# A re-planned instruction order, 45 fewer idle matmuls and three output stores in halves, in a fused RWKV attention and SMELU feed-forward kernel

## The chip, the core and the metric

The kernel runs on one core of one Trainium2 chip as a single launch. The metric is the device time of one execution in microseconds (us). The kernel before has a median of 182.87 us over 5 runs (182.36 to 184.13).

## What is computed

A recurrent attention without softmax (RWKV) over 4 batches, 8 heads, 768 steps and 48 channels per head, then a feed-forward layer with the SMELU activation over the 3072 rows of 384 channels that come out of it.

```python
batch, n_heads, seq, head_dim = (4, 8, 768, 48)
n_tokens, d_model, d_ff = (3072, 384, 2048)
...
for t in range(S):
    cur = np.einsum('bhd,bhe->bhde', u[None] * kt, vt)
    y[:, :, t] = np.einsum('bhd,bhde->bhe', rt, state + cur)
    state = w[None, :, :, None] * state + np.einsum('bhd,bhe->bhde', kt, vt)
...
h = x @ w_in
g = np.where(pos, h, np.where(neg, 0.0, (h + beta) ** 2 / (4.0 * beta)))
return (g @ w_out).astype(np.float32)
```

Here pos is h >= 1, neg is h <= -1, and beta is 1. All inputs and the output are float32.

## The kernel before

**Units.** The sequence is cut into 6 chunks of 128 steps. A chunk of one batch is a unit, so there are 24 units, numbered chunk by chunk, and unit i belongs to batch i % 4. Two units make a feed-forward block m of 256 rows (12 blocks).

**Names.** Each piece of work has a short name, used below and in the order string. For unit i:

- ld:K:i, ld:R:i, ld:V:i load 192 KB each with DMAs issued by SyncE's queue (SP).
- Kw and Rw multiply K and R by tables of decay powers and write both into one bf16 tile RKW (line 282). KU1 and KU2 form u*K*R, and dg sums it per head (line 297); Vb is V in bf16; VD is V times dg.
- trp transposes RKW on TensorE (line 306) and trc copies the result out; from unit 8 on tr does it by a DMA.
- at computes the scores A (line 322), mk masks their two halves on VectorE (line 326), y is the matmul with V (lines 334 to 343), x its copy out of PSUM, xp and xT its transpose and copy, and xs a sum of squares.
- st is the update of the state (line 378), Ta, Td and Tb its addition, decay and bf16 copy.

For a block m: L1:m:n is a group of the first feed-forward matmul (line 401) and sm the squared activation that takes it from PSUM (line 412, ScalarE). For blocks 0 and 1 the two units are done apart, as L1:m:n:u. L2:m:u:n is two matmuls of the second layer (line 432), oc copies unit u's output from PSUM, so stores it (line 447). The last unit's output (L2:11:1) is done in two column halves, and its second half is stored by ScalarE's queue.

**Weights.** w_in and w_out come as four slices each, loaded by GpSimd's (POOL's) own DMA queue with a cast to bf16: gi:0 to gi:3 and go:0 to go:3. li:z and lo:z stand for their landing and issue nothing. Before each of these loads a copy of one element on POOL (lines 460, 465, 470) waits for a certain other load: gi:0 to gi:3 for K1, R1, V1 and K2, go:0 to go:3 for K3, R3, V3 and K4. L1:0:2 needs slice li:2, L2:m:u:4 and 5 need lo:2, L2:m:u:6 and 7 need lo:3.

**Order.** The string ORDER (lines 16 to 89) holds all pieces of work in one list. A loop at the end (line 638) emits them in that order, so that each engine's and each queue's own sequence is what the list leaves for it; engines wait for each other by semaphores. A suffix such as @DVE picks another engine for a piece. The costs and due times that stand beside each op in the code take no part in the run. The token warm*n emits n matmuls of an identity matrix with itself (line 240), whose result nobody reads; there are 126 of them.

**End.** The last thing that SP does is to wait for the semaphores of its eight DMA lanes, one after the other (line 650). DMAs issued by SP and ScalarE take the eight lanes in turn.

Of the kernel before, what the change touches and what calls it, by code (L numbers as in the profile page):

```python
# [689 lines left out]
```

## Time and profile before

| | |
|---|---|
| median of 5 runs | 182.87 us |
| the profiled execution | 182.68 us, of which the profile's span is 180.8 us |
| TensorE (PE) busy | 168.3 us, 93% of the span |
| VectorE (DVE), ScalarE (ACT), GpSimd (POOL) busy | 120.4, 105.8 and 108.5 us |
| mean granted TensorE clock | 0.997 |
| idle matmuls (line 240) | 126, 10.6 us of busy time |
| from 39 to 100 us | PE busy 61.0 of 61 us, DVE 53.1, POOL 53.7, ACT 42.8 |
| DMA engines' mean share in the first 40 us | 0.84 to 1.19 |

How to read it: the span runs from the first instruction of the program to the last. A row of the timeline has its start, its length, the engine, the line, the operation, the tiles it writes and reads, how many instructions were merged, and in brackets how long the engine had been idle before and what ended that. Times of matmuls are pipelined: the time from one start to the next is shorter than the duration of one. PEld is the weight load in TensorE, SPq the instruction queue of SyncE.

### The profile page before, as it was taken

How to read it: one execution, taken by the hardware profiler on the slowest of the kernel's cores; microseconds unless marked ns; L12 is line 12 of the kernel's file. 1: busy time of each engine (PE TensorE's matmuls, PEld its weight loads, DVE VectorE, ACT ScalarE, POOL GpSimd, SP SyncE). 2: the span in 40 equal slices, each digit the busy share in tenths (PEclk: the TensorE clock that was granted, in tenths of full speed). 3: DMA queues.
4: the chain of work that ended last, by engine and by line, in shares of the span. 5: the costliest groups of instructions: out<-in, count | busy, mean ns of one | idle time of the engine just before them, and what ended most of it. 6: DMA issues, size and time to landing. Idle time of an engine off the chain costs nothing.

```text
span 180.8 us, 4899 instructions
## 1 busy us (share of the span) xinstructions
PE 168.3 (93%) x1891; PEld 129.7 (72%) x1891; DVE 120.4 (67%) x330; ACT 105.8 (59%) x225; POOL 108.5 (60%) x151
## 2 busy tenths in 40 slices
PE   5987587999999999999999999999999999999980
PEld 3876477767878777787778777777777776887670
DVE  2276762459996899879868999889869675100220
ACT  3406296526859549588737567777956551674300
POOL 7797389754999797999988998922950000000000
PEclk9999999999999999999999999999999999999998
DMA  5999979999989999996999788999943023020131
GB/s 95 221 190 206 194 113 219 205 175 187 232 202 206 202 198 237 199 189 91 247 202 181 172 135 183 224 184 204 200 113 99 4 54 98 4 86 0 39 108 49
DMA packets 103424, 27.79 MB, mean 154 GB/s; under 512 B 96481, under 2 KB 103394, under 8 KB 103394
## 3 DMA queue, kind: packets, MB, share of 16 engines
q1 hardware_dynamic: 99538, 24.16, 66.8%
q0 software_dynamic: 3712, 3.15, 11.2%
q8 instruction: 17, 0.28, 0.6%
q14 instruction: 13, 0.11, 0.2%
q10 hardware_dynamic: 144, 0.10, 0.2%
HBM read 20.65 MB, written 4.72 MB: 140 GB/s over the span
## 4 chain that ended last, share of the span: by engine, by line
PE 80%; SPq 12%; DMA 4%; issue 0%; DVE 0%; ACT 0%
PE o_p L432 35%; PE h_p L401 32%; SPq L278 12%; PE A L322 4%; DMA R<-in_r_dram 4%; PE y L337 2%; PE y L334 2%; PE st L378 2%; PE tr L306 1%; PE xp L362 1%; DVE RKW L282 0%; PE y L343 0%; SPq L243 0%; PE n_p L488 0%; PE o_p L240 0%
## 5 line engine op out<-in xcount | busy, mean ns | idle before, releaser
L412 ACT ACTIVATE gT<-h_p 128x512 bf16<-128x512 f32 x96 | 56.8, 596 | 39.3 <-PE h_p L401 37.5
L401 PE MATMUL h_p<-xT,w_in_sb 128*128 128x256 bf16 (+1 forms) x672 | 75.1, 257 | 2.6 <-DMA w_in_sb<-in_moe_w_in_dram 2.2
L432 PE MATMUL o_p<-w_out_sb,gT 128*128 128x384 bf16 (+1 forms) x400 | 75.9, 320 | 0.0
L401 PEld LDWEIGHTS <-w_in_sb 128*128 128x128 bf16 x672 | 56.9, 98 | 13.0 <-DMA w_in_sb<-in_moe_w_in_dram 2.4
L432 PEld LDWEIGHTS <-gT 128*128 128x128 bf16 x400 | 36.4, 98 | 15.6
L326 DVE TENSOR_TENSOR AT<-A,umask 128x512 bf16<-128x512 f32 x48 | 31.4, 685 | 8.9 <-PE A L322 8.7
L354 DVE SCALAR_TENSOR_TENSOR x<-Vb,dg,y 128x48 bf16<-128x48 bf16 x144 | 26.7, 258 | 5.3 <-PE y L337 5.2
L282 POOL TENSOR_TENSOR RKW<-K,Winv 128x384 bf16<-128x384 f32 x21 | 22.0, 1051 | 3.3 <-DMA K<-in_k_dram 1.7
L182 DVE COPY o_sb<-o_p 128x384 f32<-128x384 f32 (+1 forms) x20 | 10.6, 542 | 19.9 <-PE o_p L432 19.7
L293 POOL TENSOR_TENSOR KU<-KU,R 128x384 f32<-128x384 f32 x20 | 20.3, 1017 | 5.0 <-DMA R<-in_r_dram 2.3
L182 ACT CAST Tbd<-T 48x192 bf16<-48x192 f32 x40 | 13.9, 349 | 14.7 <-DVE T L386 9.5
L290 POOL TENSOR_TENSOR KU<-K,u_bc 128x384 f32<-128x384 f32 x22 | 22.0, 1003 | 0.0
L372 ACT ACTIVATE x<-x 128x384 bf16<-128x384 bf16 x24 | 12.5, 520 | 4.9 <-DVE x L354 3.5
L282 POOL TENSOR_TENSOR RKW<-R,Wpow 128x384 bf16<-128x384 f32 x14 | 14.0, 1000 | 0.3 <-DMA R<-in_r_dram 0.3
L182 POOL CAST Vb<-V 128x384 bf16<-128x384 f32 x22 | 11.3, 517 | 4.7 <-PE h_p L401 2.5
L297 DVE TENSOR_REDUCE dg<-KU 128x8 f32<-128x384 f32 x24 | 12.9, 544 | 0.7 <-POOL KU L293 0.5
L282 DVE TENSOR_TENSOR RKW<-R,Wpow 128x384 bf16<-128x384 f32 x10 | 7.8, 779 | 7.6 <-DMA R<-in_r_dram 7.6
L384 DVE TENSOR_TENSOR T<-T,st 48x192 f32<-48x192 f32 x32 | 11.2, 350 | 2.5 <-PE st L378 1.9
L389 POOL TENSOR_TENSOR T<-T,wc 128x192 f32<-128x192 f32 x16 | 9.1, 568 | 6.1 <-DVE T L384 6.0
L240 PE MATMUL w_p<-ident 128*128 128x128 bf16 x120 | 10.6, 253 | 0.0
L240 PEld LDWEIGHTS <-ident 128*128 128x128 bf16 x126 | 9.6, 116 | 0.3
L322 PEld LDWEIGHTS <-RK 48*128 48x128 bf16 x192 | 5.4, 94 | 6.0 <-issue 4.9
(74 smaller groups left out, 145.8 us busy)
## 6 DMA issues: line engine op xcount, KB each, us to landing
K<-in_k_dram SPq DMA_DIRECT2D x24, 192.0 KB, 3.8
R<-in_r_dram SPq DMA_DIRECT2D x24, 192.0 KB, 4.1
V<-in_v_dram SPq DMA_DIRECT2D x24, 192.0 KB, 3.9
out_dram<-o_sb SPq DMA_DIRECT2D x23, 192.0 KB, 2.5
w_in_sb<-in_moe_w_in_dram POOLq DMA_DIRECT2D x4, 384.0 KB, 8.1
w_out_sb<-in_moe_w_out_dram POOLq DMA_DIRECT2D x4, 384.0 KB, 7.7
RK<-RKW SPq DMA_TRANSPOSE x16, 3.5
w_bc<-in_w_dram SPq DMA_DIRECT2D x1, 192.0 KB, 3.6
```

The lines of the kernel that those rows point to most:

```text
L182: (eng.copy if eng is nc.scalar else eng.tensor_copy)(to, src)
L240: mm(spare[0][:, d_out:], ident, ident, start=False, stop=False, skip_group_check=True)
L278: nc.sync.dma_start(out=t[name, i], in_=src[b, :, c * C : (c + 1) * C, :].rearrange("h s d -> s h d"))
L282: at_engine((name + "w", i)).tensor_mul(RKW[i % RING["W"]][:, off : off + H, 0:D], t[name, i], tab)
L290: at_engine(("KU1", i)).tensor_mul(t["KU", i], t["K", i], u3)
L293: at_engine(("KU2", i)).tensor_mul(t["KU", i], t["KU", i], t["R", i])
L297: nc.vector.reduce_sum(t["dg", i], t["KU", i], axis=AX)
L326: nc.vector.tensor_mul(t["AT", i, s], t["A", i][s], umask4)
L354: nc.vector.scalar_tensor_tensor(x[:, h * D : (h + 1) * D], t["Vb", i][:, h, :], t["dg", i][:, h : h + 1], t["y", i][:, h, :], op0=ALU.mul ...
L401: mm(h_p[:, f, :], w_in_sb[:, kk, (nf * n + f) * 128 : (nf * n + f + 1) * 128], xT[m][:, :, kk, :] if u_ is None else xT[m][:, u_, kk, :], ...
L412: nc.scalar.activation(g, h_p, AF.Square, bias=0.5, scale=0.5)
L432: mm(t["o", m, u, part_], t["g", m][:, f, u * C : (u + 1) * C], w_out_sb[:, f, e], start=(f == 0), stop=(f == nN - 1),)
```

## The change

- The whole ORDER is another one. It holds the same pieces of work; 15 of them sit on another engine (Kw:0, Kw:1, KU1:3, KU2:3 and KU2:22 go from POOL to DVE, Rw:9 from DVE to POOL, VD:2 from DVE to POOL, trc:3 from ACT and xT:0 from ACT to DVE, Vb:4, Vb:15, Vb:17 from POOL to ACT, and oc:4:0, oc:5:1 and oc:11:0 from DVE to ACT).
- 81 idle matmuls stand in place of 126: 7 and 30 before the first transposes (12 and 41 before), 2, 11, 9 and 17 up to the first group of layer 1 (11, 12, 17, 2), none around at:1 (7 and 7), 5 ahead of L1:0:1:1 (2 and 9), and none ahead of L2:0:1:4 (6).
- The stores of units 20, 21 and 22 go out as two DMAs of half the columns each.
- The tile dg has 12 buffers in place of 4.
- Scores of two units in one piece of work are provided for from unit PAIR = 24 on; there is no unit 24, so no instruction comes from it.

```diff
 ORDER = """
-w u ld:K:0 ld:K:1 ln warm*12 ub tab:K ld:R:0 Kw:0 wt uc ld:V:1 tab:R KU1:0 dec ld:R:1 gi:0 ld:V:0 Rw:0 KU2:0
-warm*41 trp:0 ld:R:2 trc:0@DVE gi:1 li:0 dg:0 warm*11 at:0 Vb:0 mk:0:1 VD:0@POOL st:0 mk:0:0 gi:2 ld:K:2
-Ta:0:1 warm*12 y:0 Ta:0:0 Tb:0:1 Rw:1 Tb:0:0 ld:V:2 Kw:1 x:0@DVE warm*17 xp:0 xs:0 li:2 gi:3 trp:1 xT:0
-trc:1 Kw:2@DVE warm*2 L1:0:0:0 Rw:2 KU1:1@DVE sm:0:0:0 li:1 warm*7 at:1 KU2:1 mk:1:0 KU1:2 warm*7 L1:0:2:0
-dg:1 mk:1:1 li:3 Vb:1 sm:0:2:0 trp:2 KU2:2@DVE trc:2 VD:1 st:1 dg:2 Vb:2 L1:0:1:0 Ta:1:0 ld:K:3 y:1 VD:2
-sm:0:1:0 at:2 Ta:1:1 x:1 ld:K:4 mk:2:1 st:2 Tb:1:0 xs:1 L1:0:3:0 mk:2:0 ld:R:3 go:0 Tb:1:1 xp:1 Ta:2:0
-sm:0:3:0 Ta:2:1 ld:V:3 warm*2 y:2 xT:1 Kw:4 x:2@DVE Tb:2:0 ld:R:4 Tb:2:1 go:1 warm*9 L1:0:1:1 xs:2 xp:2 lo:0
-sm:0:1:1 L1:0:0:1 go:2 L1:0:2:1 sm:0:0:1 Rw:4 xT:2 L1:0:3:1 Kw:3 sm:0:2:1 lo:1 trp:4 sm:0:3:1 Rw:3@POOL
-L1:1:0:0 trc:4@DVE L1:1:1:0 KU1:3 sm:1:0:0 L2:0:1:0 sm:1:1:0 L2:0:0:0 lo:2 go:3 at:4 L2:0:1:1 mk:4:1 KU1:4
-L1:1:2:0 mk:4:0 trp:3 sm:1:2:0 KU2:4 L2:0:1:2 lo:3 L2:0:1:3 trc:3 L1:1:3:0 KU2:3 dg:4 sm:1:3:0 Vb:3 dg:3
-warm*6 L2:0:1:4 L2:0:1:5 ld:K:5 L2:0:0:1 VD:3@POOL L2:0:0:2 at:3 ld:V:4 L2:0:0:3 mk:3:0 L2:0:0:4 st:3
-L2:0:1:6 mk:3:1 ld:K:6 L2:0:1:7 KU1:5 L2:0:0:5 Ta:3:0 L2:0:0:6 Ta:3:1 ld:R:5 Tb:3:0 L2:0:0:7 Vb:4 oc:0:1 y:3
-Tb:3:1 VD:4 L2:1:0:0 ld:V:5 x:3 L2:1:0:1 oc:0:0 xs:3 L2:1:0:2 Kw:5@DVE st:4 ld:R:6 y:4 Rw:5 xp:3 x:4
...
-sm:11:7 L2:10:1:6 oc:10:0 L2:10:1:7 L2:11:1:0:1 oc:10:1 L2:11:0:0 L2:11:0:1 L2:11:0:2 L2:11:0:3 so:10:0
-L2:11:1:0:0 L2:11:1:1:1 L2:11:1:2:1 L2:11:0:4 so:10:1 L2:11:0:5 L2:11:0:6 L2:11:0:7 L2:11:1:1:0 L2:11:1:2:0
-oc:11:0 L2:11:1:3:0 L2:11:1:4:0 L2:11:1:5:0 L2:11:1:6:0 L2:11:1:7:0 L2:11:1:3:1 L2:11:1:4:1 oc:11:1:0
-L2:11:1:5:1 L2:11:1:6:1 L2:11:1:7:1 so:11:0 oc:11:1:1 so:11:1:0
+w u ld:K:0 ld:K:1 ln warm*7 ub tab:K ld:R:0 Kw:0@DVE wt uc ld:V:1 tab:R gi:0 dec ld:V:0 KU1:0 ld:R:1 Rw:0
+KU2:0 warm*30 trp:0 li:0 trc:0@DVE Vb:0 dg:0 gi:1 warm*2 at:0 st:0 mk:0:1 VD:0@POOL ld:R:2 mk:0:0 gi:2
+Ta:0:0 ld:K:2 warm*11 y:0 Ta:0:1 Tb:0:0 Rw:1 Tb:0:1 ld:V:2 Kw:1@DVE Vb:1 x:0@DVE warm*9 trp:1 li:2 gi:3 st:1
+xs:0 xp:0 Ta:1:1 trc:1 Rw:2 KU1:2 xT:0@DVE Ta:1:0 li:1 Tb:1:0 KU1:1@DVE warm*17 L1:0:0:0 Kw:2@DVE at:1
+sm:0:0:0 KU2:2@DVE L1:0:2:0 mk:1:0 KU2:1 li:3 dg:2 sm:0:2:0 trp:2 Vb:2 mk:1:1 VD:2@POOL trc:2 dg:1 st:2
+L1:0:1:0 VD:1 ld:K:3 Ta:2:0 sm:0:1:0 at:2 y:1 Tb:2:0 mk:2:1 ld:R:3 x:1 mk:2:0 L1:0:3:0 xs:1 ld:R:4 go:0
+sm:0:3:0 Ta:2:1 ld:K:4 Tb:1:1 xp:1 go:1 y:2 Tb:2:1 xT:1 x:2@DVE ld:V:3 Kw:3 xs:2 warm*5 L1:0:1:1 lo:0 Kw:4
+L1:0:0:1 sm:0:1:1 Rw:4 xp:2 sm:0:0:1 L1:0:2:1 go:2 xT:2 L1:0:3:1 lo:1 sm:0:2:1 Rw:3@POOL trp:4 sm:0:3:1
+L1:1:0:0 trc:4@DVE go:3 L1:1:1:0 sm:1:0:0 KU1:3@DVE trp:3 lo:2 sm:1:1:0 at:4 KU2:3@DVE L2:0:1:0 trc:3@DVE
+KU1:4 L2:0:1:1 L1:1:2:0 mk:4:0 KU2:4 L2:0:0:0 dg:3 sm:1:2:0 lo:3 L1:1:3:0 mk:4:1 VD:3@POOL L2:0:1:2 sm:1:3:0
+L2:0:1:3 dg:4 L2:0:0:1 Vb:3 L2:0:0:2 L2:0:1:4 L2:0:1:5 ld:K:5 at:3 L2:0:0:3 mk:3:1 ld:V:4 L2:0:0:4 L2:0:0:5
+mk:3:0 st:3 L2:0:1:6 ld:K:6 L2:0:1:7 Ta:3:1 KU1:5 L2:0:0:6 Ta:3:0 Tb:3:1 L2:0:0:7 oc:0:1 ld:R:5 Tb:3:0 y:3
...
+L2:10:0:7 sm:11:7 L2:10:1:6 oc:10:0 L2:10:1:7 L2:11:1:0:1 oc:10:1 L2:11:0:0 L2:11:0:1 L2:11:0:2 L2:11:0:3
+so:10:0 L2:11:1:0:0 L2:11:1:1:1 L2:11:0:4 so:10:1 L2:11:0:5 L2:11:0:6 L2:11:1:1:0 L2:11:1:2:1 L2:11:1:2:0
+L2:11:1:3:0 L2:11:0:7 L2:11:1:4:0 L2:11:1:5:0 oc:11:0@ACT L2:11:1:6:0 L2:11:1:7:0 L2:11:1:3:1 L2:11:1:4:1
+oc:11:1:0 L2:11:1:5:1 L2:11:1:6:1 L2:11:1:7:1 oc:11:1:1 so:11:0 so:11:1:0
 """
...
@@ -124,12 +124,13 @@
     nN = d_ff // 128
     nP = nN // 2
     UB = 2
+    SPLIT = (20, 21, 22)
     MT = UB * C
     NB = NU // UB
     NQ = 4
     FQ, TQ = d_ff // NQ, nN // NQ
     LIM = 0.95
-    PE_T, PE_X, PE_D, ONE = 8, 14, 6, 2
+    PE_T, PE_X, PE_D, ONE, PAIR = 8, 14, 6, 2, 24
     mm = nc.tensor.matmul
     AX = mybir.AxisListType.X
 
@@ -293,7 +294,7 @@
         at_engine(("KU2", i)).tensor_mul(t["KU", i], t["KU", i], t["R", i])
 
     def diag(i):
-        t["dg", i] = work.tile([128, H], F32, name="dg", tag="dg", bufs=4)
+        t["dg", i] = work.tile([128, H], F32, name="dg", tag="dg", bufs=12)
         nc.vector.reduce_sum(t["dg", i], t["KU", i], axis=AX)
 
     def vdiag(i):
@@ -444,6 +445,10 @@
     def store(m, u, part_=None, queue=nc.sync):
         c, b = at_of(m * UB + u)
         t0 = b * S + c * C
+        if part_ is None and m * UB + u in SPLIT:
+            for z in range(2):
+                queue.dma_start(out=out[t0 : t0 + C, part(z)], in_=t["o_sb", m, u, part_][:, part(z)])
+            return
         queue.dma_start(out=out[t0 : t0 + C, part(part_)], in_=t["o_sb", m, u, part_])
 
     w_in_src = moe_w_in.rearrange("(ko ki) n -> ki ko n", ki=128)
@@ -507,6 +512,16 @@
 
 
     P, L0 = 13.0, 17.0
+    RTs = {}
+
+
+    def at_key(i):
+        return ("at", i if i < PAIR else i - i % 2)
+
+    def scores_of_two(i):
+        scores(i)
+        scores(i + 1)
+
     op("w", "SP", 0.6, load_w)
     op("u", "SP", 0.1, load_u)
     op("ub", "PE", 1.3, spread_u, ["u"], 0, [("a", ["uc"])])
@@ -545,7 +560,7 @@
         if i < PE_D:
             op(("VD", i), "DVE", 0.5, (vdiag, i), [("dg", i), ("ld", "V", i)], d + 4, [("VD", [("y", i)])], port=True,
                alt={"POOL": (1.0, True)})
-        rk = ("RK", [("at", i)] + [("y", i)] * (c > 0))
+        rk = ("RK", [at_key(i)] + [("y", i)] * (c > 0))
         if pe:
             op(("trp", i), "PE", 0.47, (tr_pe, i), [("Kw", i), ("Rw", i)], d + 2, [("a", [("trc", i)])])
             op(("trc", i), "ACT", 1.02, (tr_copy, i), [("trp", i)], d + 2, [rk], alt={"DVE": (0.68, False)})
@@ -553,9 +568,14 @@
         else:
             op(("tr", i), "SP", 1.6, (tr_dma, i), [("Kw", i), ("Rw", i)], d + 2, [rk], land=3.5)
             RT = ("tr", i)
-        op(("at", i), "PE", 0.45, (scores, i), [RT], d + 3, [("a", [("mk", i, s)]) for s in range(2)])
+        RTs[i] = RT
+        if i < PAIR:
+            op(("at", i), "PE", 0.45, (scores, i), [RT], d + 3, [("a", [("mk", i, s)]) for s in range(2)])
+        elif i % 2:
+            op(at_key(i), "PE", 0.66, (scores_of_two, i - 1), [RTs[i - 1], RT], d + 1,
+               [("a", [("mk", z, s)]) for z in (i - 1, i) for s in range(2)])
         for s in range(2):
-            op(("mk", i, s), "DVE", 0.69, (mask, i, s), [("at", i)], d + 3, [("AT" + str(s), [("y", i)])])
+            op(("mk", i, s), "DVE", 0.69, (mask, i, s), [at_key(i)], d + 3, [("AT" + str(s), [("y", i)])])
         needs = [("mk", i, s) for s in range(2)] + [("Vb", i)]
         needs += [("VD", i)] * (i < PE_D) + [("Tb", i - B, s) for s in range(2) if c > 0]
         op(("y", i), "PE", 0.22 + 0.17 * (c > 0) + 0.19 * (i < PE_D), (ymm, i), needs, d + 5, [("a", [("x", i)])])
```

## The prediction

> **What bounds the kernel now.** I read the page first, then the chain of waits up to 40 us, the busy time by stretches, the waits of TensorE, the timeline of the first 36 us with the DMA landings, and last the instructions at the end.
>
> By stretches (the columns are the busy times of PE, PEld, DVE, ACT and POOL):
>
> ```profile
> 15.00:20.50 5.50, 2.95 (x47) 2.45 (x47) 4.11 (x9) 2.61 (x5) 3.29 (x5) 1.00 1.23 198
> 20.50:30.40 9.90, 8.32 (x147) 7.54 (x147) 4.82 (x11) 8.28 (x19) 7.05 (x12) 1.00 1.00 166
> 30.40:39.00 8.60, 8.57 (x110) 6.46 (x111) 3.89 (x7) 3.29 (x5) 6.40 (x9) 1.00 1.24 204
> 39.00:100.00 61.00, 61.00 (x716) 46.97 (x714) 53.07 (x154) 42.80 (x96) 53.71 (x66) 1.00 1.03 196
> ```
>
> From 39 us on TensorE never stops. Whatever the new order does there costs nothing unless it makes a hole in PE; DVE and POOL have about 8 us of slack in those 61, ACT 18. So the time is decided before 39 us and after PE's last matmul. In the first 39 us the DMA engines are full and PE has holes. Its waits, and the two rows of the timeline that matter most:
>
> ```profile
> PE h_p L401 <- DMA w_in_sb<-in_moe_w_in_dram: 2.2, 1, 2.2
> ...
> PE xp L362 <- DVE x L182: 0.9, 1, 0.9
> PE tr L306 <- DVE RKW L282: 0.8, 1, 0.8
> ```
>
> ```profile
> 9.60 0.61 PE L306 MATMUL tr<-ident,RKW 128*128 128x128 bf16 x8
> ...
> 20.57 0.84 PE L401 MATMUL h_p<-xT,w_in_sb 128*128 128x128 bf16 x12 [2.19 <-DMA w_in_sb<-in_moe_w_in_dram]
> ```
>
> The second is L1:0:2:0: it waits for li:2, whose last byte lands at 20.53. The chain then goes back to loads:
>
> ```profile
> 19.77 3.39 SPq L278
> 23.16 0.04 issue
> 23.20 6.53 DMA R<-in_r_dram
> 29.73 0.02 issue
> 29.75 0.63 DVE RKW L282
> 30.38 0.05 issue
> 30.43 0.40 PE tr L306 x4
> ```
>
> So trp:4 waits for R4, the 16th load of SP, which lands 6.5 us after its issue began because go:0's slice goes ahead of it. A last gate is not in the waits, it is so small: L2:0:1:6 starts at 38.84, and its slice lo:3 landed at 38.79. From 38.84 on all is PE work.
>
> **Part 1: idle matmuls before the first transposes.** The 41 run from 5.71 to 9.60, 95 ns each (107 ns until 9.09, 56 ns after). R0's weighing ends at 8.03, so trp:0 could start earlier. With 30: 5.71 + 30 x 0.107 = 8.92; then eight transposes, two at 0.107 and six at 0.056, end at 9.47 in place of 10.05. That is 0.58 us earlier for trp:0, and DVE's trc:0, dg:0 and masks move with it. None of it reaches the end by itself: PE waits at 20.57 for li:2, whatever came before. The 25 fewer idle matmuls from trp:0 to L1:0:2:0 (39 for 64, some 56 ns each) also lie ahead of that gate and are worth nothing, and if this cover were gone, 1.4 us at most. Past the gate 12 go: those ahead of L1:0:1:1 (11 to 5) are hidden under ACT's chain (part 3); the 6 ahead of L2:0:1:4 give 6 x 0.056 = 0.34 us, if lo:3 allows.
>
> PE's clock: the longest hole before, 2.35 us up to 20.57, is followed by matmuls at 56 ns and a granted clock of 1.00. With no idle matmuls around at:1 the hole before li:2 grows to about 2.8 us (at:1 done near 17.7, li:2 at 20.5). The Trainium skill, "TensorE: Matmul & The Clock Gate", section "Why this matters for your kernels", speaks against taking them out: it asks for no idle gap over some 3 us and says that one idle window (about 3.4 us, by Part 1 of the page) halves the clock. By that rule a longer hole could cost one more window at half speed, an estimate of 1.7 us; no run here shows such a fall. I stay with the row: 0, as 2.8 is nearer to 2.35 than to any gap that this trace shows to be punished.
>
> **Part 2: the w_in slices.** Kw:0 goes from POOL to DVE, and gi:0 becomes POOL's first piece. It waits only for K1, which lands at 6.15, so its DMA is issued at about 6.4 in place of 8.02, 1.6 us earlier. Its first packets came 2.2 us after the issue, and once it ran it took nearly everything: from 11 to 12 us its queue moved 143 KB and SP's queue 14 KB. R1 is now the eighth load, not the seventh (V0 is ahead of it). It landed at 8.91; the eighth slot landed at 9.77 with no slice running. With gi:0 from 8.6 on, R1 falls into its start, as K2 did before (landing 0.5 to 2.9 us after the first packet): 10.6 to 11.5. POOL's gi:1 waits for R1, and behind it are VD:0 (which y:0 needs), gi:2, Vb:1 and gi:3. gi:1 is then issued at about 11 (10.05 before), gi:2 at about 13 (12.38), gi:3 near 14.5 (14.65). Each slice streams for 2.5 us, and gi:1 to gi:3 ran one after the other from 13.5 to 21.5, so these issue times change nothing: li:2 at 20.5. Bounds: 1.6 us earlier (the whole row of slices follows gi:0) to 0.7 us later (R1 at 11.5 and more). I take 0.
>
> **Part 3: from li:2 to trp:3.** at:2 now stands ahead of y:1, and at:2 waits for trc:2 on ACT until about 23.05, so x:1 starts at 24.05 (23.33 before). ACT then has x:1 0.5, xs:1 0.7, sm:0:3:0 0.6, Tb 2 x 0.35, xT:1 0.48 to do: L1:0:1:1 at 27.05, 1.07 us later than the 25.98 of before. The four groups and xp:2 take it to 29.9, trp:4 to 30.35. Before, trp:4's second half ended at 30.65 for R4's sake. R4 and K4 are now SP's 14th and 15th loads (24.01 to 25.78 by those slots), so that this wait of 1.0 us is gone, and the 1.07 us fill its place: a gain of 0.3, not 1.
>
> What is late next: V3 is now the 16th load, the slot that landed at 29.73 behind go:0. And POOL has go:0, go:1, Kw:3, Kw:4, **go:2, Rw:3, go:3**: go:2's one-element copy waits for V3, and Rw:3 and go:3 are queued behind it. PE has trp:3 right after L1:1:1:0, near 31.7, where it came at 34.24 before, and trp:3 needs Rw:3. go:1 is issued about 1 us earlier than 25.34 (it no longer follows Kw:4), which narrows the gap of 1.2 us between the two slices in which R4 came in. So V3 lands between 28.5 (the load comes before the slice) and 32.5 (after all of go:1); I take 30.2, near the slot's own 29.73. Then go:2's copy and issue (0.2 + 0.8), Rw:3 (1.0): trp:3 starts at 32.25 and ends at 32.7. Before, PE stood at 32.16 with trp:3 (0.45) still to do: equal within 0.1.
>
> **Part 4: the w_out slices.** From trp:3 to L2:0:1:6 PE has at:4 and at:3 0.66, twelve L2 pairs 3.91, two L1 groups 1.32 and st:3 0.17, together 6.06: it arrives at 38.76, with L2:0:0:5 (0.33) done that came later before. lo:2 (issue 30.4 plus 5.3 to 8.6, as the eight slices took) is needed at 36.6, lo:3 (issue 32.4, with only go:2 ahead) at 38.8; by the shorter latencies both are in time, by the longest lo:3 is 2 us late. Net: 38.76 - 38.84 - 0.33 = -0.41 us. The 0.34 of idle matmuls is within it.
>
> **Part 5: the end.** SP walks its eight lanes in order. After the last landing at 178.39 it still had four of these:
>
> ```profile
> L650 SPq EVENT_SEMAPHORE  x4: 17/17/17, 178.4 to 178.6; - x4
> ```
>
> They start 67 ns apart. The issues of SP and ACT number 125 (72 loads, 2 of w and u, 26 transposes, 25 stores): 125 = 15 x 8 + 5, so the last store is on the fifth lane. With 128 it is on the eighth, and three steps go: 3 x 0.067 = -0.20 us. The price is three more issues of 0.33 us on SP. The pair of so:11:0 begins 0.7 us before PE's end (oc:11:0 on ACT 0.5 us sooner than that), and behind it only the last unit's first half waits, perhaps 0.2 us later than its 175.26; it must land before the other half, issued at 176.05. Hidden, or +0.2 if not. If the lanes are dealt otherwise, 0.
>
> The other changes (dg's buffers, the changes of engine from unit 4 on, the order of the middle) lie under dense PE work: 0, with up to +0.5 if an order of the middle starves PE.
>
> **Sum.** -0.41 - 0.20 = -0.6 us on the profiled 182.68 gives 182.1. That execution is 0.19 below the median, so 182.3. This case's own range, from lo:3 and V3 a microsecond either way: 181.4 to 183.6. A difference under 1% (1.8 us) can't be told from none here.
>
> **Rivals.** Slower: V3 comes after all of go:1, or later still as go:1 itself moves. POOL stands in go:2's copy, Rw:3 waits behind it, PE in trp:3. Each microsecond of V3 past 30.2 is one on the end; at 32.5 it is +2.3 - 0.6 = +1.7, and lo:3 moves along (up to 2.0 more): 183.7 to 185.6, about 184.5. It decides from V3 at 30.8 on. For it: R4 took 6.5 us in that slot. Against: go:1 can only start once go:0 is through.
>
> Faster: the 1.6 us of gi:0 pass through. R1 lands before the slice takes over, li:2 and li:3 come a microsecond and a half earlier, K3 (which go:0 waits for) and V3 too: -1.6 - 0.6 = -2.2, 180.7, from 180.2 to 181.3. Against it: the same bytes go through full DMA engines.
>
> Only the lanes: all gates stay and just 0.2 is left, 182.7; inside the forecast's range.
>
> **How the numbers follow.** Forecast (with the last rival) 0.6, slower rival 0.22, faster rival 0.18. The range takes half of each rival: 180.9 to 184.5. Faster by over 1% (below 181.0): most of the faster rival, 0.17. Slower by over 1% (above 184.7): half of the slower rival and a starved middle, 0.17. Within: 0.66.
>
> **What would show it.** The first transposes near 8.9; L1:0:2:0 at 20.5 again behind w_in; no wait for R ahead of trp:4, but a PE wait for POOL's RKW near 32; one lane step after the last landing, not four. I am wrong if L1:0:2:0 starts before 19.5, if trp:3 waits past 33, or if PE has holes after 40 us.

## The result and the profile after

| | before | after |
|---|---|---|
| median | 182.76 us (79 runs, 181.46 to 186.41) | 183.78 us (42 runs, 182.34 to 186.25) |
| ratio to before | | 1.005, 95% interval 1.0034 to 1.0066 |
| the profiled execution | 182.68 us, span 180.8 | 185.05 us, span 182.9 |
| mean granted clock in it | 0.997 | 0.981 |

The change made the kernel slower by half a per cent, 0.9 us. That is inside the 1% that the prediction could not tell from none, but with this many runs it is resolved. The profiled execution of after is 1.3 us above its median: what it shows happened, but its sizes are not the average's. Ratios leave out executions more than 1.5% above the fastest of the same kernel, and the profiled ones of e2 (185.87 us) and e6 (186.15 us) are such executions, so what they show is a mechanism and not a size.

The page of after, PE's busy tenths and the granted clock in 40 slices of 4.6 us:

```profile
PE   4946497999999999999999999999999999999990
PEclk9996869999999999999999999999999999999999
```

Before, every slice but the last had a 9 in the clock's row. Now the fourth, fifth and sixth slice have 6, 8 and 6, and PE's own row has 4, 6 and 4 from the third on. The same stretches as in the prediction (PE, PEld, DVE, ACT, POOL busy, then the granted clock, DMA share and GB/s):

```profile
15.00:20.50 5.50, 5.24 (x62) 4.87 (x61) 3.22 (x8) 2.25 (x5) 3.86 (x8) 0.69 1.13 185
20.50:30.40 9.90, 6.42 (x91) 5.63 (x90) 6.26 (x13) 5.83 (x13) 9.68 (x15) 0.83 1.24 199
30.40:39.00 8.60, 8.60 (x133) 7.55 (x130) 4.52 (x8) 5.26 (x11) 3.18 (x5) 1.00 1.12 181
39.00:100.00 61.00, 61.00 (x710) 46.56 (x708) 51.61 (x146) 41.80 (x94) 51.44 (x64) 1.00 0.94 190
```

From 20.50 to 30.40 PE did 91 matmuls where it did 147 before, at a mean clock of 0.83. From 39 us on it never stops, as before. TensorE's waits in the first 45 us (total, times, longest), the two longest:

```profile
PE y L344 <- POOL VD L302: 2.9, 1, 2.9
PE h_p L402 <- DMA w_in_sb<-in_moe_w_in_dram: 2.4, 1, 2.4
```

The wait for R4 ahead of trp:4 is gone. The first wait is new, and the timeline has its cause:

```profile
8.84 0.61 PE L307 MATMUL tr<-ident,RKW 128*128 128x128 bf16 x8
...
12.90 0.57 POOL L465 COPY hold<-R 1x1 f32<-1x1 f32 x1 [2.70 <-DMA R<-in_r_dram]
...
15.27 0.34 PE L344 MATMUL y<-VD,ident 128*128 128x384 bf16 x1 [2.87 <-POOL VD L302]
...
16.36 1.06 PE L307 MATMUL tr<-ident,RKW 128*128 128x128 bf16 x8
```

The second row is gi:1's one-element copy: POOL stood in it until R1 landed, 12.85 (8.91 before). VD:0 is queued behind it, y:0's last matmul needs VD:0, and PE stood from 12.40 to 15.27. Then trp:1 ran at half speed: the same eight transposes that took 0.61 as trp:0 took 1.06. The chain of waits goes through it:

```profile
13.47 0.76 POOL w_in_sb L470
14.25 0.96 POOL VD L302
15.21 0.08 POOL hold L465
15.29 7.59 DMA w_in_sb<-in_moe_w_in_dram
22.88 0.05 issue
22.92 1.46 PE h_p L402 x12
```

gi:2 was issued at 15.29 (12.38 before), li:2 landed at 22.88 (20.53), L1:0:2:0 started at 22.92 (20.57) and itself ran at half speed (1.46 for twelve matmuls, 0.84 before).

The lane semaphores that SP still walked after the last landing, 180.69:

```profile
L670 SPq EVENT_SEMAPHORE  x4: 17/17/17, 180.7 to 180.9; - x4
```

Still four. ScalarE's store is on the eighth lane, as meant, but SP came to its walk only at 180.39 and went through all eight lanes without standing at one for long: here SP itself was late, not a store.

To set executions beside each other I cut each at three points: the start of L1:0:2:0 (the **gate**), the start of L2:0:1:6 (the **middle** lies between), and PE's last matmul (the **end** is from there to the end of the span). Before: gate 20.57, middle 18.26, end 5.11. After: 22.92, 18.47, 4.93.

### The profile page after: what moved, and what is told of

It reads as the page before. It is cut to its first block, busy times and chain, and to the rows that moved or that the text cites. A ratio compares the mean times of both kernels' runs of the same rounds, so it can differ in the third digit from the quotient of the medians.

```text
span 182.9 us, 4793 instructions
## 1 busy us (share of the span) xinstructions
PE 167.9 (92%) x1846; PEld 129.6 (71%) x1846; DVE 119.5 (65%) x332; ACT 107.6 (59%) x229; POOL 104.5 (57%) x145
## 4 chain that ended last, share of the span: by engine, by line
PE 83%; DMA 8%; SPq 3%; ACT 2%; POOL 1%; issue 0%
PE h_p L402 35%; PE o_p L433 35%; DMA w_in_sb<-in_moe_w_in_dram 4%; PE A L323 4%; DMA R<-in_r_dram 4%; PE y L338 2%; SPq L279 2%; PE y L335 2%; PE st L379 2%; PE tr L307 2%; PE xp L363 1%; POOL VD L302 1%; POOL w_in_sb L470 0%; PE y L344 0%; POOL hold L465 0%
## 5 line engine op out<-in xcount | busy, mean ns | idle before, releaser
L183 DVE COPY o_sb<-o_p 128x384 f32<-128x384 f32 (+1 forms) x17 | 9.1, 540 | 22.2 <-PE o_p L433 22.0
L294 POOL TENSOR_TENSOR KU<-KU,R 128x384 f32<-128x384 f32 x18 | 19.3, 1071 | 3.5 <-DVE KU L291 1.6
L283 POOL TENSOR_TENSOR RKW<-K,Winv 128x384 bf16<-128x384 f32 x19 | 19.4, 1024 | 3.2 <-DMA K<-in_k_dram 3.1
L283 POOL TENSOR_TENSOR RKW<-R,Wpow 128x384 bf16<-128x384 f32 x15 | 15.0, 1000 | 0.2 <-DMA R<-in_r_dram 0.2
L183 POOL CAST Vb<-V 128x384 bf16<-128x384 f32 x19 | 10.1, 531 | 5.3 <-DVE x L355 3.5
L323 PE MATMUL A<-RK 48*128 48x128 bf16 x192 | 9.4, 219 | 0.7 <-DVE RK L183 0.7
L241 PEld LDWEIGHTS <-ident 128*128 128x128 bf16 x81 | 7.4, 130 | 3.1 <-issue 3.0
L338 PE MATMUL y<-Vb,AT 128*128 128x48 bf16 x192 | 8.7, 184 | 0.5 <-DVE AT L327 0.5
```

Of the source, the lines that this page charges most:

```text
L183: (eng.copy if eng is nc.scalar else eng.tensor_copy)(to, src)
L283: at_engine((name + "w", i)).tensor_mul(RKW[i % RING["W"]][:, off : off + H, 0:D], t[name, i], tab)
L294: at_engine(("KU2", i)).tensor_mul(t["KU", i], t["KU", i], t["R", i])
L323: mm(t["A", i][s][:, p, :], KT[rows[s], p, :], RT[rows[s], p, :], start=True, stop=True)
```

## The experiments

Three theories. **A, the clock:** 45 idle matmuls fewer let the granted clock fall, and half speed between 15 and 26 us costs a microsecond or more. **B, gi:0:** issued 1.6 us earlier, its slice starves the load in flight, R1 comes late, POOL's row of slices with it. **C, the end:** the split stores with the last unit's new order make the end longer. A fourth thing is the new order of the middle, which may gain. Edits are shown as the changed tokens of ORDER; the kernel that was changed is named. Ratios are to the kernel before on the same chip, with 95% intervals.

**e1, after with 74 more idle matmuls** (44 ahead of y:0, 30 ahead of L1:0:2:0).

```diff
-Ta:0:0 ld:K:2 warm*11 y:0
+Ta:0:0 ld:K:2 warm*55 y:0
...
-sm:0:0:0 KU2:2@DVE L1:0:2:0
+sm:0:0:0 KU2:2@DVE warm*30 L1:0:2:0
```

> The changed kernel with 44 more idle matmuls ahead of y:0 (55 for 11) and 30 new ones ahead of L1:0:2:0, so that TensorE is busy in both of its long holes; the order of everything else is the changed kernel's. Theory A, the clock: the loss comes from the granted clock, which fell to half from 15.4 to 18.9 and from 22.3 to 25.7 us in the changed kernel. Then the mean granted clock returns to 0.99 or more, L1:0:2:0 still starts near 22.9 behind w_in, but the work after it runs at 56 ns and PE's end comes about 1.2 us sooner: ratio to the kernel before 0.997 to 1.000. Theory B, the order of the loads (R1 late, so gi:1, VD:0 and gi:2 late): the clock returns as well, but what bounds is w_in and then the DMAs, and the ratio stays at 1.003 to 1.007.

182.99 us, ratio 1.0019 (0.9983 to 1.0055). Full clock from 8.2 us on, gate 21.06, middle 17.48: 1.0 less than after, and 0.8 less than before. The end was 5.63. The time lies between the two forecasts and decides nothing; the middle speaks for A, and at full clock the new order of the middle is better than the old one.

**e2, after with ld:R:1 ahead of ld:V:0.**

```diff
-gi:0 dec ld:V:0 KU1:0 ld:R:1 Rw:0
+gi:0 dec ld:R:1 KU1:0 ld:V:0 Rw:0
```

> The changed kernel with R1 loaded ahead of V0 again, as in the kernel before; nothing else differs. Theory B: R1 lands near 9.5 and not at 12.9, gi:1 is issued at about 10 to 10.5 and not 13.4, VD:0 ends near 12, the 3 us hole inside y:0 goes, li:2 lands at 20 to 20.5, and the ratio to the kernel before is 0.995 to 0.999; the clock stays up in the first hole. Theory A alone: the holes get shorter only as far as y:0, at:1 to L1:0:2:0 still has no idle matmuls, and a fall of the clock stays near 20 us with a ratio of about 1.002.

183.70 us, 1.0037 (0.9997 to 1.0077). R1 landed at 8.97, as expected, and yet the gate was 23.35. V0 was now the eighth load, and it landed at 12.94:

```profile
13.00 0.50 POOL L181 CAST Vb<-V 128x384 bf16<-128x384 f32 x1 [3.30 <-DMA V<-in_v_dram]
```

Vb:0 stands ahead of gi:1 on POOL. So B as first put, that R1 is the point, fell: gi:0's slice starves whichever load is eighth, and POOL waits for that load either way.

**e3, before with 81 idle matmuls, placed as in after.**

```diff
-ld:K:1 ln warm*12 ub
+ld:K:1 ln warm*7 ub
...
-mk:1:0 KU1:2 warm*7 L1:0:2:0
+mk:1:0 KU1:2 L1:0:2:0
...
```

> The kernel before with the changed kernel's idle matmuls in its own order: 7, 30, 2, 11, 9, 17, none around at:1, 5 ahead of L1:0:1:1 and none ahead of L2:0:1:4, 81 in all. Theory A: with 14 fewer around at:1 and 9 fewer ahead of y:0 the clock falls in the hole up to li:2 near 20 us, the mean granted clock is 0.98 to 0.99 and the ratio 1.003 to 1.007. Theory B: li:2 lands at 20.5 as before, whatever PE does, and the ratio is 0.998 to 1.001.

183.49 us, 1.0007 (0.9973 to 1.0042): against A's range, no cost that this shows, though the clock was at half from 19.45 to 26.28. Gate 21.09; from there to L1:0:1:1 7.25 (before 5.41), but to L2:0:1:6 only 18.65 (18.26). Of the 1.84 us lost by then 0.39 is left: PE's wait for R4 at trp:4 (0.85 before) was gone, so that part of the loss came out of waits that the old order has anyway. The new order no longer has that wait.

**e4, before with the split stores alone** (the code of the change, nothing else).

```diff
+    SPLIT = (20, 21, 22)
...
+        if part_ is None and m * UB + u in SPLIT:
+            for z in range(2):
+                queue.dma_start(out=out[t0 : t0 + C, part(z)], in_=t["o_sb", m, u, part_][:, part(z)])
+            return
```

> The kernel before with the stores of units 20 to 22 in halves and nothing else. Both theories: the last store moves from the fifth lane to the eighth, three lane steps of 67 ns go, 0.2 us: ratio 0.998 to 1.000, and from PE's last matmul to the end of the span 4.9 us in place of 5.1. A rival: the longer queue on SP holds up the last unit's first half and eats the gain, 5.1 us again.

182.47 us, 0.9985 (0.9946 to 1.0024). The last landing, 178.63, was followed by one lane step, 178.64; before there were four, 0.2 us. But it came 3.27 us after PE's end, against 2.73. End 5.33, against 5.11. So the lanes are dealt as the prediction had it, and the 0.2 us went; in this execution the landing took more. The ratio shows neither a gain nor a loss.

**e5, after with gi:0 back behind KU2:0.**

```diff
-tab:R gi:0 dec ld:V:0 KU1:0 ld:R:1 Rw:0 KU2:0 warm*30
+tab:R dec ld:V:0 KU1:0 ld:R:1 Rw:0 KU2:0 gi:0 warm*30
```

> The changed kernel with gi:0 behind KU1:0 and KU2:0 on POOL (issued near 8.3 us and not at 6.4, the time of the kernel before); its 81 idle matmuls stay. Theory B, in the form that the run with R1 ahead of V0 left of it (gi:0's slice starves whatever load is the eighth, and POOL stands behind that load): R1 and V0 both land by 10, gi:1 is issued near 10.3, VD:0 ends near 12, there is no hole inside y:0, L1:0:2:0 starts at 20 to 20.6, PE's end is 1.5 to 2 us sooner than in the changed kernel's profile; ratio to the kernel before 0.998 to 1.002. Theory A: idle matmuls are as few as before, so the clock still falls, at the latest in the hole up to L1:0:2:0, mean granted clock 0.98 to 0.99, and the ratio stays over 1.002.

183.78 us, 1.0034 (1.0006 to 1.0063). R1 landed at 9.60, y:0's hole was gone, the gate was 21.38. Then the clock still fell (21.7 to 25.1 us), and the middle was 18.68. So gi:0's early place explains the gate in after's profiled execution, not the average: e5 takes 0.0016 off after's 1.005, less than the intervals are wide.

**e6, after with gi:1 behind VD:0.**

```diff
-Vb:0 dg:0 gi:1 warm*2 at:0 st:0 mk:0:1 VD:0@POOL ld:R:2
+Vb:0 dg:0 warm*2 at:0 st:0 mk:0:1 VD:0@POOL gi:1 ld:R:2
```

> The changed kernel with VD:0 ahead of gi:1 on POOL; gi:0 stays early. The hole inside y:0 comes only from VD:0 standing behind gi:1: y:0 ends near 12.5, the clock does not fall at 15 us; gi:1 is still issued near 13 when R1 lands, gi:2 about 1 us sooner than 15.3. If the late slices bound (theory B), L1:0:2:0 starts at 22 to 22.9 and the ratio is 1.002 to 1.005; if the first fall of the clock was what cost (theory A), L1:0:2:0 is still near 22 but the ratio is under 1.001.

184.17 us, 1.0064 (1.0029 to 1.01). The gate came at 20.10, but L2:0:1:6 at 41.98, as late as with a gate of 23. POOL's and PE's waits from 25 to 43 us:

```profile
POOL hold L463 <- DMA V<-in_v_dram: 4.8, 1, 4.8
```
```profile
PE tr L305 <- POOL RKW L281: 1.8, 1, 1.8
PE o_p L431 <- DMA w_out_sb<-in_moe_w_out_dram: 1.2, 1, 1.2
```

V3 landed at 31.58 here (26.68 in after). That is the slower rival of the prediction to the letter: V3, go:2's copy, Rw:3, trp:3, then lo:3. It exists, past the point given for it (30.8), but it is not what made the profiled execution of after slow.

**e7 and e8, two mixtures.** e7: after with gi:0 late, 41 more idle matmuls, whole stores and the last unit's old order. e8: e1 with whole stores and the old last unit.

```diff
-x:0@DVE warm*9 trp:1
+x:0@DVE warm*20 trp:1
...
-KU2:2@DVE L1:0:2:0
+KU2:2@DVE warm*30 L1:0:2:0
...
-    SPLIT = (20, 21, 22)
+    SPLIT = ()
```

> The changed kernel with gi:0 behind KU2:0, 30 idle matmuls ahead of L1:0:2:0 and 11 more ahead of trp:1, no split stores, and the order of the last unit as in the kernel before (oc:11:0 on DVE). If A, B and the tail each cost what was seen, this is the new order without its losses: L1:0:2:0 near 20.3, L2:0:1:6 at 38 or sooner, the tail from PE's end 5.1 us, the mean clock 0.993 or more, ratio 0.993 to 0.997. If the new middle is worth nothing, 1.000.

> The changed kernel with the idle matmuls of the first experiment (55 ahead of y:0, 30 ahead of L1:0:2:0), no split stores and the order of the last unit as in the kernel before; gi:0 stays early. It tells the tail apart: SP's issue of the last unit's first half takes 0.33 us again and starts 0.4 us ahead of PE's end, and from PE's end to the span's end it is 5.1 us, where the first experiment had 5.6; ratio 0.997 to 1.000, some 0.3% under the first experiment. If the stores' split is harmless, the tail is longer by 0.2 us than with it.

e7: 182.35 us, 0.996 (0.9924 to 0.9996), mean clock 0.994, although its profiled execution has one fall (gate 21.49, middle 18.48). e8: 183.45 us, 1.0029 (0.9995 to 1.0063), where 0.997 to 1.000 was expected: its clock was full (mean 0.998), and it is no faster than e1 (1.0019), though its profiled end was 4.86, against e1's 5.63.

**e9, e10 and e11.** e9 is e7 with 70 for 30 idle matmuls ahead of L1:0:2:0. e10 is e9 with y:1 ahead of at:2 again. e11 is e9 with the split stores and the new last unit.

```diff
-sm:0:1:0 at:2 y:1 Tb:2:0
+sm:0:1:0 y:1 at:2 Tb:2:0
```

> The kernel of the run with gi:0 late, more idle matmuls and the old last unit (0.996), now with 70 idle matmuls ahead of L1:0:2:0 in place of 30. Its clock fell at 22.5 us after a stretch in which TensorE was busy for a third. Theory A: with the hole filled to about 21.2 us no stretch of 3.4 us is under 0.6 busy, the mean granted clock is 0.996 or more in nearly all executions, from L1:0:2:0 to L2:0:1:6 it takes 17.5 us and not 18.5, and the ratio to the kernel before is 0.990 to 0.995. If the clock there is hidden under w_in and the loads, the ratio stays at 0.996.

> The same kernel with 70 idle matmuls, and y:1 ahead of at:2 on TensorE, as in the kernel before. The prediction priced the new order (at:2 waits for trc:2, so x:1 and ACT's chain are later) at 1.07 us up to L1:0:1:1; at full clock the new order took 6.1 us from L1:0:2:0 to L1:0:1:1 where the kernel before took 5.4. If that price is real, it is 5.4 to 5.6 here, and the ratio is 0.001 to 0.004 under the run with 70 idle matmuls alone; if later waits (K4, w_out) take it back, the ratio is the same.

> The kernel with 70 idle matmuls, but with the changed kernel's split stores and its order of the last unit (oc:11:0 on ACT). Theory C, the tail: the split stores put six pieces into the last microseconds, SP issues the last unit's first half at PE's end and not 0.4 us ahead of it, and the pieces land later: from PE's end to the span's end 5.3 to 5.6 us, ratio 0.002 to 0.003 over the run with 70 idle matmuls alone. The prediction's view, three lane steps saved: 0.001 under it.

e9: 182.74 us, 0.9981 (0.995 to 1.0012), above the 0.990 to 0.995 expected. e10: 182.34, 0.9984 (0.9948 to 1.002). e11: 183.38, 1.0033 (0.9995 to 1.0072). The clock stayed full, but 70 were too many: li:2 had landed and the idle matmuls themselves held the gate at 21.81 to 21.86 in e9 and e10. From the gate to L1:0:1:1 e10 needed 5.76, e9 6.10: at:2 first costs 0.34, not 1.07. e11 against e9 speaks for C: 0.0052 more, though e11's one profiled end was a good one (4.85). Against A: e11 is e5 with 81 more idle matmuls and nothing else, and the two are equal (1.0033 and 1.0034).

**e12, after with whole stores and the last unit's old order.**

```diff
-L2:11:1:5:0 oc:11:0@ACT L2:11:1:6:0
+L2:11:1:5:0 L2:11:1:6:0
...
-L2:11:1:7:1 oc:11:1:1 so:11:0 so:11:1:0
+L2:11:1:7:1 so:11:0 oc:11:1:1 so:11:1:0
...
-    SPLIT = (20, 21, 22)
+    SPLIT = ()
```

> The changed kernel with unsplit stores and the old order of the last unit, and nothing else undone. Theory C: its tail is 4.8 to 5.1 us and the ratio 1.002 to 1.004 to the kernel before, where the changed kernel has 1.005. If the tail costs nothing, 1.005 to 1.006; the clock falls as in the changed kernel (mean 0.98 to 0.99) in either case.

183.10 us, 1.0007 (0.9971 to 1.0043), 0.0043 under after: for C. Against A again: e8 is e12 with 74 more idle matmuls, and it was not faster (1.0029 and 1.0007). Up to the last unit e12 is after, and yet its profiled execution had the gate at 19.25, 3.7 us ahead of after's: R1 landed at 10.18, not at 12.85. One order, two gates: what an early gi:0 does is not settled by the order. The early gate bought little: with a fall from 18.98 and V3 at 29.72, e12 came to L2:0:1:6 at 38.79, where before was at 38.84.

**e13, before with the 73 idle matmuls behind trp:0 taken out.**

```diff
-li:0 dg:0 warm*11 at:0
+li:0 dg:0 at:0
...
-Tb:2:1 go:1 warm*9 L1:0:1:1
+Tb:2:1 go:1 L1:0:1:1
...
```

> The kernel before without any idle matmul after the first transposes: 73 taken out, the 12 and 41 ahead of them kept. A doubled dose of theory A. In the profiles so far a stretch of 3.4 us with TensorE busy for 0.52 of it or less was followed by half the clock in the next one, and one with 0.61 or more was not. Here the stretches from 9 to 20 us are at 0.1 to 0.5, so the clock is at half for most of 12 to 26 us; theory A prices a half-speed stretch past li:2 at 1.0 us, hidden ones ahead of it at nothing: L1:0:2:0 to L2:0:1:6 takes 19.3 us and more in place of 18.3, mean clock 0.96 to 0.975, ratio 1.005 to 1.010. If w_in and R4 hide it, the ratio stays under 1.002.

183.25 us, 1.0055 (1.0021 to 1.0089), mean clock 0.966. For A, in the old order too, if enough is taken out. Its profiled execution shows only 0.3 us of that (span 181.1), so where the rest goes stays open.

**e14, before with the three stores in quarters.**

```diff
+            for z in range(4):
+                e = slice(z * d_out // 4, (z + 1) * d_out // 4)
+                queue.dma_start(out=out[t0 : t0 + C, e], in_=t["o_sb", m, u, part_][:, e])
```

> The kernel before with the stores of units 20 to 22 in four pieces each: 9 more DMAs, twice and more the dose of the split. Theory C (more pieces land later, on the slowest of the 16 DMA engines): the last landing 3.5 to 4.5 us after PE's end in place of 2.9, from PE's end to the span's end 5.6 to 6.5 us, ratio 1.003 to 1.007. If the pieces are harmless and only the lanes count, 5.0 to 5.2 us and 0.999 to 1.001.

186.06 us (6 runs), 1.0175 (1.0121 to 1.0229), end 8.83. This is no larger dose of the same thing: ScalarE's last copy of the output waited for the landing of an earlier store and began only 2.8 us after PE's end. It says nothing on the halves.

**e15, before with the new last unit and whole stores; e16, before with 40 idle matmuls for 7 ahead of L1:0:2:0.**

```diff
-L2:11:1:5:0 L2:11:1:6:0
+L2:11:1:5:0 oc:11:0@ACT L2:11:1:6:0
...
-L2:11:1:7:1 so:11:0 oc:11:1:1 so:11:1:0
+L2:11:1:7:1 oc:11:1:1 so:11:0 so:11:1:0
```
```diff
-KU1:2 warm*7 L1:0:2:0
+KU1:2 warm*40 L1:0:2:0
```

> The kernel before with the changed kernel's order of the last unit (oc:11:0 on ACT, L2:11:0:7 later) and whole stores. It parts theory C in two. If the later copy is what holds up SP, the issue of the last unit's first half starts at PE's end or its first piece later than 0.4 us ahead of it, and the tail is 5.2 us or more, ratio 1.001 to 1.003. If only the pieces do it, the tail is 4.8 to 5.1 and the ratio 0.999 to 1.001.

> The kernel before with 40 idle matmuls ahead of L1:0:2:0 in place of 7, 159 in all. Its stretches of 3.4 us stood at 0.62 to 0.63, just over the shares that were followed by a fall, and some executions of it had a mean granted clock of 0.983 to 0.990. Theory A: those executions go, the mean clock is 0.993 or more in all, and the ratio is 0.996 to 0.999. If the clock costs nothing there, 1.000.

e15: 182.80 us, 1.0021 (0.9981 to 1.0061), end 5.92. e16: 182.55 us, 1.0003 (0.9971 to 1.0034). The first is unclear in time, but its profile bears on the cause: SP issued the last unit's first half 0.40 us ahead of PE's end, as in before, and no extra store stood in its queue; still the last landing came 3.64 us after PE's end, against 2.73. The second shows no gain from a still fuller clock in before.

**e17 and e18, the clean pair.** e17: after with gi:0 late, y:1 ahead of at:2, whole stores, the old last unit, and 66 more idle matmuls (11 ahead of trp:1, 55 ahead of L1:0:2:0, a number that fits the hole). e18: the same with after's own 81.

```diff
-x:0@DVE warm*9 trp:1
+x:0@DVE warm*20 trp:1
...
-KU2:2@DVE L1:0:2:0
+KU2:2@DVE warm*55 L1:0:2:0
```

> The changed kernel with gi:0 behind KU2:0, y:1 ahead of at:2, whole stores and the old last unit, 11 more idle matmuls ahead of trp:1 and 55 ahead of L1:0:2:0 (70 held L1:0:2:0 up by some 0.3 us: they ended at 21.8, li:2 landed at 21.4). All three causes are undone. L1:0:2:0 at 21.0 to 21.5, 17.1 us from there to L2:0:1:6, mean clock 0.995 or more, ratio 0.993 to 0.998. If the new order is worth nothing over the old one, 0.999 to 1.001.

> The same kernel with the changed kernel's 81 idle matmuls, so none in the hole ahead of L1:0:2:0: theory A alone, with the gate and the tail undone. Theory A: the clock falls after that hole in most executions (mean 0.98 to 0.99), from L1:0:2:0 to L2:0:1:6 it takes 18.1 to 18.3 us in place of 17.1, and the ratio is 0.003 to 0.006 over that of the run with 55 more. If the idle matmuls cost as much as they save, the ratios are equal.

e17: 182.12 us (181.73 to 182.54), 0.9957 (0.9933 to 0.9981): faster than both kernels. e18: 183.41 us (182.45 to 184.48), 1.003 (1.0 to 1.006). Nothing but 66 idle matmuls lies between them, they ran on the same chip in turn, and the kernel that does more work is faster by 1.3 us. The stretch with the wait for li:2 and the one behind it in e18, and the stretch with that wait in e17 (columns as in the result):

```profile
17.41:20.82 3.41, 0.42 (x10) 0.22 (x8) 3.38 (x7) 0.60 (x1) 2.95 (x3) 1.00 1.21 191
20.82:24.23 3.41, 3.02 (x30) 3.02 (x31) 0.51 (x2) 1.26 (x2) 0.94 (x2) 0.50 0.75 138
```
```profile
18.63:22.04 3.41, 2.77 (x51) 2.60 (x48) 1.74 (x4) 0.10 (x1) 1.70 (x4) 1.00 1.21 196
```

In e18 PE was busy 0.42 of 3.41 us there, and the next stretch was at half clock; in e17 it was busy 2.77, and the clock held. PE's longest waits, first e17 (15 to 45 us), then e18 (12 to 45 us):

```profile
PE h_p L400 <- ACT xT L181: 0.7, 1, 0.7
PE h_p L400 <- DMA w_in_sb<-in_moe_w_in_dram: 0.6, 1, 0.6
```
```profile
PE h_p L400 <- DMA w_in_sb<-in_moe_w_in_dram: 3.4, 1, 3.4
PE o_p L431 <- DMA w_out_sb<-in_moe_w_out_dram: 1.1, 1, 1.1
```

Their gates differ by 0.15 only (21.06 and 21.21). Then e18 is at half clock, and L1:0:1:1 comes at 28.30, not 26.84. The 1.46 us go on into POOL's queue (go:2 is issued at 30.71, not 29.23), and in this execution lo:3, at 40.92, added a wait of 1.1: L2:0:1:6 at 40.97, not 38.59.

## Why the prediction was wrong

It said 182.3 us, 0.6 less than the kernel before; the runs say 0.9 more. The measured 183.78 lies above its own range (181.4 to 183.6) and inside the one that takes in half of each rival (180.9 to 184.5), but neither rival is what happened. The account that the runs give:

- **Order and engines, at full clock: about -0.8 us.** e17 against before, 0.9957. It has the old end, a late gi:0 and y:1 first, so this is what the rest of the new order is worth when nothing spoils it. The profiled executions agree (181.86 and 182.68), 0.3 of it behind PE's last matmul (4.81 and 5.11). e10, which differs from e17 in 15 idle matmuls alone, says 0.3 less, with an interval on both sides of 0.
- **Fewer idle matmuls: 1.3 us in the clean pair, some 0.5 in after itself.** e18 against e17, whose intervals do not meet. The other three pairs that differ in idle matmuls alone say 0.6 (after against e1), 0.0 (e5 against e11) and -0.4 us (e12 against e8), none of them clear of the intervals. After's own executions tell it without another kernel: of the 38 in its ratio, the 18 with a mean granted clock of 0.973 to 0.981 have a median of 183.95 us, the 20 with 0.986 and more have 183.41.
- **The end: about +0.4 us.** Over the profiled executions of the new order the end is 5.26 on average with split stores and the new last unit (six, 4.85 to 5.63) and 4.88 with whole stores and the old one (seven, 4.81 to 5.01). The pairs say 0.8 (e12 against after), 0.9 (e9 against e11) and -0.2 us (e8 against e1).
- **gi:0 and at:2: near 0** (gi:0 early: +0.3 by after against e5, +0.9 by e8 against e9 and -0.3 by e1 against e11, where the idle matmuls differ a little too; at:2: nothing by e10; all within the intervals).

With the clean pair's 1.3 these add up to the measured 0.9, but that it fits so well is luck: with the 0.5 of after's own executions the sum is 0.1. What is shown is that taking the idle matmuls out lets the clock fall, that this costs time, and that the order without the falls is faster than before. How the 0.9 divides among the clock, the end and the early gi:0 stays open, and so does where a part of it comes from.

**Part 1 failed in its clock term, the 0.** The prediction weighed a hole against holes: 2.8 us expected, 2.35 before at full clock (the row itself says 2.19), so no fall. It also miscounted what is taken out between trp:0 and L1:0:2:0: not 25 idle matmuls (39 for 64) but 17 (39 for 56). A single hole was the wrong thing to look at. The granted clock moves in stretches of 3.41 us, and what counts is how busy PE is within one. After's four such stretches from 12.02 on, then one of e16 that kept its clock, then before's two in the same place (columns as above):

```profile
12.02:15.44 3.42, 0.55 (x10) 0.40 (x11) 2.22 (x4) 0.70 (x2) 2.52 (x5) 1.00 1.09 203
15.44:18.85 3.41, 3.41 (x35) 3.41 (x34) 1.60 (x3) 1.63 (x3) 3.04 (x5) 0.50 1.07 176
18.85:22.27 3.42, 1.68 (x30) 1.36 (x28) 3.39 (x9) 0.95 (x2) 2.16 (x3) 1.00 1.23 202
22.27:25.68 3.41, 2.76 (x28) 2.76 (x29) 1.46 (x4) 1.00 (x2) 3.39 (x7) 0.50 1.22 207
```
```profile
28.05:31.46 3.41, 1.85 (x31) 1.56 (x28) 3.15 (x1) 2.33 (x5) 3.41 (x5) 1.00 1.13 172
```
```profile
15.91:19.32 3.41, 2.23 (x38) 1.72 (x35) 2.02 (x5) 1.89 (x3) 2.69 (x4) 1.00 1.23 203
19.32:22.73 3.41, 2.16 (x44) 2.16 (x45) 2.40 (x6) 1.27 (x2) 0.15 (x1) 1.00 1.09 184
```

PE busy 0.55 of 3.42 us: half clock next. Busy 1.68 of 3.42, 49%: half clock next, though the hole in it, from 20.5 to 22.9, was no longer than 2.4 us. Busy 1.85 of 3.41, 54%: full clock next. Before itself ran here at 2.23 and 2.16 of 3.41, 65 and 63%, with its idle matmuls; with after's 81, in its own order, it fell too (e3). That the idle matmuls "also lie ahead of that gate and are worth nothing" was right for their time and wrong for the clock.

The Trainium skill's page "TensorE: Matmul & The Clock Gate" spoke against this edit, and the prediction set it aside. Its window of 3413 ns (Part 1) is the 3.41 of these rows. Its condition for the slow state, "after ≥1 idle window", is milder than what the rows show: a window half busy was enough, and the rows decide.

The prediction's estimate by that page, 1.7 us for a window at half speed, was nearer than 0. From the gate to L1:0:1:1 it takes 6.10 to 6.12 us in e1, e8, e9 and e11, at full clock, and 7.10 to 7.32 in after, e2, e5, e6, e7 and e12, which have a fall there: a fall costs 1.0 to 1.2. In after, e2, e5 and e7 the whole middle keeps that loss (18.5 to 18.7, against 17.5); in e6 and e12, where V3 comes late, and in e18, later waits add to it (21.88, 19.54 and 19.75).

**Part 2: the terms were in the wrong place.** trp:0 came at 8.84, as said (near 8.9). gi:0 was issued at 6.39 (6.4). But R1 landed at 12.85, not between 10.6 and 11.5, VD:0 waited for it, and li:2 came 2.35 later, outside the bounds of -1.6 to +0.7. (The slices did not run from 13.5 to 21.5 in before either, as the prediction read it: gi:1 to gi:3 landed at 18.10, 20.53 and 23.04.) Over the executions with gi:0 early and after's order of loads the gate follows R1: 10.18 and 19.25 (e12), 10.76 and 20.10 (e6), 11.07 and 21.06 (e1), 12.33 and 21.80 (e8), 12.85 and 22.92 (after). The value taken, 0, lies within e5's interval, but these gates span 3.7 us where the bounds spanned 2.3, and the faster rival's early gate was there once, 1.3 us early, without an earlier end of the middle (e12).

**Part 3.** The wait for R4 went, as said. At:2 first was priced at 1.07 and cost 0.34. V3 was put at 30.2 and landed at 26.68: SP issued it at 19.24, where the load in that slot had gone out at 23.20. So the slower rival's mechanism stayed away from after, and with it the wait for POOL's RKW near 32 that the prediction named as a sign; e6 shows it whole, at V3 31.58.

**Part 4.** The middle at full clock was 0.8 shorter, with L2:0:0:5 (0.33) done in it besides: more than the 0.41 given. From L2:0:1:6 on there is no hole in either kernel, so that the many changes after 40 us were indeed worth nothing (136.83 us from there to PE's end before, 136.56 after, which has done the 0.33 of L2:0:0:5 by then).

**Part 5 had the lanes right and the price wrong.** One step is left after the last landing in e2, e4 and e5, as said. But the last landing moved out. With whole stores and the old last unit it comes 2.7 to 3.0 us after PE's end; with split stores it came 2.74 (after), 2.81 (e11), 3.27 (e4), 3.60 (e5), 3.66 (e2), 3.71 (e6) and 3.86 us (e1) after it. In before, the last unit's first half was issued 0.40 us ahead of PE's end, in after at PE's end, and there its issue took 1.28 us, not 0.33. SP's instructions from 174 us on, in after:

```profile
174.02 3.84 SPq L450 DMA_DIRECT2D out_dram<-o_sb  x3
177.95 1.28 SPq L452 DMA_DIRECT2D out_dram<-o_sb  x1
```

SP begins its walk 1.16 us after its last issue ends (before: 175.59 to 176.76; after: 179.23 to 180.39), so that a long issue eats the steps that the lanes saved. That is why after still shows four. "Hidden, or +0.2 if not" was the step that failed, together with the -0.20: in the new order the end is some 0.4 us longer than with whole stores and the old last unit, not 0.2 shorter. The three issues alone did not delay the last unit (in e4 it was issued 0.40 us ahead of PE's end), and the new last unit alone, with no extra issue, had the longest end but e14's (e15, 5.92). The landings show what happens. Every store lands in sixteen parts. In before all parts of so:11:0 had landed 2.08 us after its issue, ahead of the trouble; of the last unit's first half fifteen came within 1.62 us and the sixteenth at 2.84. With oc:11:0 later, so:11:0 too is in flight then: in e15 fifteen of its parts came within 1.86 us and the sixteenth at 4.11, and the last unit's halves behind it were complete at 3.80 and 3.26. In e4 the second half of so:11:0 waited likewise for its sixteenth part (1.71 and 3.78). So one part in sixteen comes late near the end of the kernel, and the change puts one store more, or two halves, into that time. Why that part is late is not shown.

## What to carry to other kernels

Idle matmuls ahead of a wait cost no time, but they hold up the clock of what comes after the wait: before removing them, add up how busy TensorE stays in each stretch of the clock's own length (3.41 us here), not how long one hole is. A transfer that is issued earlier through a queue that takes the DMA engines over does not only come earlier; it pushes back the load that is in flight then (R1 here, from 8.91 to between 10.18 and 12.85), so look who waits for that load and what is queued behind the waiter. A shorter walk over semaphores at the end was worth 0.07 us a step here, and the stores that buy it are among the last ones, whose landings set the end. And where several causes are undone one by one, undo them all first and put one back: only that pair priced the clock clear of the noise.

## What the hardware showed that was not expected

- The granted clock follows the busy share of a stretch of 3.41 us. In the profiled executions of all these kernels, 11 stretches at full clock from 9 us on had PE busy for 49% or less, and each was followed by half clock; none with 54% or more was. Once at half, the stretch with 1.80 of 3.42 us busy (e13, from 17.43) was followed by half again, while after's from 22.27, with 2.76 of 3.41, was followed by full clock.
- The stretches do not begin at the same place in every execution (12.02 in after, 12.15 in e12, 12.50 in before), so one hole falls into them differently each time. After's executions had mean clocks from 0.964 to 1.000.
- Two executions of the same instructions (after and e12 up to the last unit) had R1 landing 2.7 us apart and the gate 3.7 us apart.
- A store's last part can come long after the others: in e1 fifteen of the sixteen parts of so:11:0's halves landed 1.45 to 1.63 and 1.56 to 1.72 us after their issue, the sixteenth at 3.39 and 3.25. Long issues on SP do not explain a long end: after and e11, with issues of 1.28 and 1.35 us, have short ones (4.93 and 4.85), e1 with 1.67 a long one (5.63), and e2 and e5, with 0.39 and 0.38, have 5.36 and 5.30.
